# An earlier gate for two loads, and list products queued behind newer work

## The chip, the cores and the metric

The kernel runs on one core of a Trainium2 chip. The metric is the time of one execution on the device in microseconds (us). The engines of the core work through one instruction list each, in order, and wait for one another by semaphores: TensorE (PE) for products and transposes, VectorE (DVE), ScalarE (ACT), GpSimd (POOL), and SyncE (SP), which here only issues DMAs. ScalarE and GpSimd issue DMAs too.

## The reference

A causal convolution along the sequence, then a mixture of experts with one expert per token. In short:

```python
w = softmax(weight, axis=-1)                         # 8 heads, 7 taps
x_pad = concatenate([zeros(B, 6, D), x], axis=1)     # x: 8 x 2880 x 192, float32
x = einsum('hk,bskhg->bshg', w, unfold(x_pad))       # causal, per head of 24 columns
g_idx = argmax(x @ w_group)                          # 4 groups
e_idx = argmax(x[g] @ w_expert[g])                   # 4 experts in the group
h = maximum(x[e] @ w1[g, e], 0)                      # 192 -> 1024
out[e] = g_w * e_w * (h @ w2[g, e])                  # 1024 -> 192, times both softmax weights
```

There are 23040 tokens and 16 experts. Every token is computed by its own expert only, so tokens have to be sorted by expert.

## The kernel before

**Units.** The tokens are cut into blocks of 120, and the blocks into units of 4, 8, 12, 8, 8, 8 blocks for the first two batches and of 12 from then on. I call a unit by its number u in the code, from 0; the eighth and ninth unit are u=7 and u=8.

**Routing of a unit** (`unit`). The block of x (`xin`, or rooms borrowed from weight buffers for u=3 to u=6) is convolved by eight products with a band matrix, one per head (L516). ScalarE copies each result out of its PSUM bank into `xc` (L525). There are three `xc` buffers: u=0 and u=1 share one, u=5 takes it next, u=2's goes to u=6, u=3's to u=7, u=5's to u=8; u=4 sits in a weight buffer. TensorE transposes `xc` (L540, L548), ScalarE copies these as `ta` and `tb` (L541, L549), the logits are products of them with the router weights (L581, L584), and ScalarE copies them to `lg` (L587). VectorE then finds the group and the expert (`mx`, `dd`, `sc`, `oh`, `ohx`, L621 to L633), counts tokens per expert within the unit (`cum`, L641), and writes the token's weight (L652), after which ScalarE issues the store of `xc` to DRAM, `xcd` (L654). Two small products with a triangle and a matrix of ones (`tri`, `ones`, L663, L664) give offsets; VectorE makes places out of them (`off`, `ends`, `pos`, `posn`, `posb`, L667 to L677) and two one-hot matrices `ohl` and `ohr` (L695, L702).

**List products** (`list_products`). One product per block of the unit (L716), with `ohl` as the weights, sorts the token numbers by expert. VectorE turns the result into `lsi` (L724, L726), GpSimd writes it into the table `idtab` (L729). For the first units the list products are put aside and run `LATE` = 8 steps later; at u=4 all that are left are run. With five units in the table, SP reads the first id list (L1228), the weights of the next experts are issued behind it, GpSimd gathers the tokens of the first slots (L816), and the expert products begin (L918, L936, L940).

**Order.** The code runs the stages of several units as generators, a step of one at a time. A scheduling layer then orders each engine's instructions by their dependencies and the order of issue; `hold` and `pin` keep an instruction in the program's order, and `issue_after` puts one behind another. Buffers that rotate add dependencies of their own.

**The gate of x.** Loads of x for u=7 to u=10 are let go late on purpose of the code: a small VectorE memset (L248) writes a corner of the `xin` buffer, and the load on SP's queue has to wait for it. u=8 begins a batch and needs a halo memset (L233) as well. `KX` = 142 is the step in which this happens for u=7 and u=8 together.

Of the kernel before, what the change touches and what calls it, by code (L numbers as in the profile page):

```python
# [24 lines left out]
BI = 2  # L25
# [4 lines left out]
LH = 32  # L30
# [7 lines left out]
def conv_moe_kernel(  # L38
# [10 lines left out]
    nc = tc.nc  # L49
# [41 lines left out]
    for b in range(B):  # L91
        k = b * NB
# [33 lines left out]
    QGB = 3  # L126
    AHEAD = 112
    LISTLAG = 8
    LATE = 8
    HOLD = 2  # L130
    LAG_S = 1
    PTURN = (4, 6)
# [21 lines left out]
    UG = [0, 5, 6, 1, 5, 8, 0, 5, 6, 0, 5, 7, 0, 5, 6, 2, 5, 10]  # L154
    SK = [8, 8, 6, 11, 10, 9, 9]
    KPRE = [60, 150, 155, 160, 162, 110]
    KX = 142
    SEV = 99
    TB = 4
    HGAP = 3  # L160
# [108 lines left out]
    for q, (p0, r0, n) in enumerate(((0, 0, P), (0, P, D2), (D2, P, D2))):  # L269
        c = min(q, 1)  # L270
# [82 lines left out]
    k = 0  # L353
    while k < E:
        n = CAPS.count(CAPS[k])
# [98 lines left out]
    GPIN = (2, 3)  # L454
    ohp_last = [None]
    list_last = [None]
    shared = []
    bands = {}

# [4 lines left out]
    def unit(u, pre=None):  # L464
# [41 lines left out]
        for h in range(H):  # L506
# [6 lines left out]
            else:  # L513
                ops = ((band, xin),)
            for i, (bb, xx) in enumerate(ops):
                nc.tensor.matmul(  # L516
                    out=ps[0:BT, 0:nb * HC], lhsT=bb[0:R, h, :], rhs=xx[0:R, :, cs],
                    start=i == 0, stop=i == len(ops) - 1,
                )
# [56 lines left out]
        def logits_of(q):  # L576
            lgp = bank("l")
            for i in range(HQ):
                o = lgp[0:BT, 2 * i * REPL * NL:2 * (i + 1) * REPL * NL].rearrange("p (j n) -> p j n", j=2)
                for j in range(2):  # L580
                    nc.tensor.matmul(  # L581
                        out=o[:, j].rearrange("p (r n) -> p r n", n=NL), lhsT=ta[:, q, 2 * i + j],
                        rhs=wr[:, 0, 0:NL].unsqueeze(1).broadcast_to([P, REPL, NL]), start=j == 0, stop=False)
                nc.tensor.matmul(  # L584
                    out=o[:, :, 0:NL], lhsT=tb[:, q, i], rhs=wrb[:, :, 0:NL], start=False, stop=True)
            read.add((u, q))
            nc.scalar.activation(  # L587
# [124 lines left out]
        def list_products():  # L712
            pl = bank("l")
            nrep = REPO if u < REPU else 1
            for k in range(nb):
                nc.tensor.matmul(  # L716
                    out=pl[:, 0:nrep * LH].rearrange("p (r n) -> p r n", r=nrep),
                    lhsT=ohl[0:Q, k // BI, :, :, k % BI].rearrange("p e l -> p (e l)"),
                    rhs=ohr[0:Q, k // BI, :, k % BI].unsqueeze(1).broadcast_to([Q, nrep, LH]),
                    start=k == 0, stop=k == nb - 1,  # L720
                )
            lv5 = rt.tile([P, LH], F32, name="lv5", bufs=1)
            lsi = rt.tile([P, LH], I32, name="lsi", bufs=4)
            nc.vector.tensor_scalar(  # L724
# [8 lines left out]
            finished(u)  # L733

        if u < NEED - 1:
            waiting.append((done[0] + LATE, list_products))
        else:
            while waiting:
                waiting.pop(0)[1]()
            list_products()  # L740
# [807 lines left out]
```

## Time and profile before

| what | us |
|---|---|
| median of 3 runs (lowest, highest) | 1089.47 (1089.16, 1090.57) |
| the profiled execution | 1089.97 |
| its span | 1088.1 |
| TensorE busy in it | 1043.7 |
| VectorE, ScalarE, GpSimd busy | 677.6, 618.4, 531.7 |

The profile is of one execution. A time in a view is counted from the start of the span. PE in a view is TensorE's products, PEld its weight loads, PEclk the share of full clock that was granted. In brackets stands how long an engine was idle before an instruction and what ended that. Source lines L in rows of before are lines of the kernel before; in the changed kernel the same lines stand 1 to 5 lines lower.

### The profile page before, as it was taken

How to read it: one execution, taken by the hardware profiler on the slowest of the kernel's cores; microseconds unless marked ns; L12 is line 12 of the kernel's file. 1: busy time of each engine (PE TensorE's matmuls, PEld its weight loads, DVE VectorE, ACT ScalarE, POOL GpSimd, SP SyncE). 2: the span in 40 equal slices, each digit the busy share in tenths (PEclk: the TensorE clock that was granted, in tenths of full speed). 3: DMA queues.
4: the chain of work that ended last, by engine and by line, in shares of the span. 5: the costliest groups of instructions: out<-in, count | busy, mean ns of one | idle time of the engine just before them, and what ended most of it. 6: DMA issues, size and time to landing. Idle time of an engine off the chain costs nothing.

```text
span 1088.1 us, 20687 instructions
## 1 busy us (share of the span) xinstructions
PE 1043.7 (96%) x7116; PEld 980.7 (90%) x7116; DVE 677.6 (62%) x1650; ACT 618.4 (57%) x1380; POOL 531.7 (49%) x677
## 2 busy tenths in 40 slices
PE   6878999999999999999999999999999999999996
PEld 5756888998999899899999999999999999999996
DVE  4667878886777766656464646556466465655652
ACT  5566687886666645545453645545455455555552
POOL 3233343543333446655554553555556656667542
PEclk9989999999999999999999999999999999999998
DMA  8866897886674343432231313133132233233200
GB/s 210 233 174 161 194 271 201 230 224 186 161 167 133 93 116 89 115 85 65 75 83 53 100 41 90 56 95 97 42 96 69 77 92 104 66 87 98 68 26 23
DMA packets 120281, 126.40 MB, mean 116 GB/s; under 512 B 20619, under 2 KB 106896, under 8 KB 120170
## 3 DMA queue, kind: packets, MB, share of 16 engines
q1 hardware_dynamic: 72682, 71.24, 24.7%
q0 software_dynamic: 24160, 35.99, 11.9%
q10 hardware_dynamic: 23328, 17.80, 6.7%
q8 instruction: 57, 0.93, 0.4%
q14 instruction: 54, 0.44, 0.1%
HBM read 89.03 MB, written 36.07 MB: 115 GB/s over the span
## 4 chain that ended last, share of the span: by engine, by line
PE 76%; DMA 7%; DVE 6%; issue 5%; ACT 3%; POOL 3%; POOLq 0%; SPq 0%; ACTq 0%; DVEq 0%
PE ph L888 26%; PE po L902 10%; PE pm L902 7%; PE ph L918 7%; PE po L906 5%; PE po L936 4%; PE pm L906 3%; PE pm L516 3%; PE po L940 2%; DMA out<-ys,idp 2%; DMA xin<-in_x 2%; PE ph L852 1%; POOL out L955 1%; POOL xg L816 1%; PE pm L540 1%
## 5 line engine op out<-in xcount | busy, mean ns | idle before, releaser
L955 POOL DMA_INDIRECT out<-ys,idp x187 | 214.2, 1146 | 258.2 <-DVE ys L965 203.9
L892 DVE SCALAR_TENSOR_TENSOR hl<-ph,hh 128x360 fp32r<-128x360 f32 (+13 forms) x328 | 189.5, 584 | 197.9 <-ACT hh L891 174.8
L891 ACT ACTIVATE hh<-ph 128x360 fp32r<-128x360 f32 (+13 forms) x328 | 166.3, 515 | 207.9 <-PE ph L888 182.4
L816 POOL DMA_INDIRECT xg<-xcd,idp x187 | 226.7, 1212 | 70.6 <-issue 36.6
L902 PE MATMUL po<-cw,hh 128*120 128x384 f32 (+6 forms) x656 | 209.9, 357 | 0.0
L888 PE MATMUL ph<-xa,wf 128*128 128x360 f32 (+13 forms) x656 | 182.3, 359 | 0.0
L888 PE MATMUL ph<-xc,wf 128*128 128x360 f32 (+13 forms) x656 | 176.4, 350 | 1.7 <-DVE xc L864 1.7
L906 PE MATMUL po<-cw,hl 128*120 128x192 f32 (+6 forms) x656 | 164.7, 251 | 0.0
L902 PE MATMUL pm<-cw,hh 128*120 128x384 f32 (+6 forms) x440 | 147.1, 356 | 0.0
L936 PE MATMUL po<-cw,hh 128*128 128x384 f32 x400 | 134.5, 386 | 0.1
L888 PEld LDWEIGHTS ph<-xc,wf 128*128 128x128 f32 x656 | 118.8, 189 | 11.1 <-DVE xc L864 1.9
L906 PEld LDWEIGHTS po<-cw,hl 128*120 128x120 f32 (+6 forms) x656 | 121.7, 186 | 3.0
L918 PE MATMUL ph<-xa,wf 128*128 128x256 f32 x600 | 118.8, 306 | 5.1 <-DVE wf L783 2.2
L902 PEld LDWEIGHTS po<-cw,hh 128*120 128x120 f32 (+6 forms) x656 | 120.4, 184 | 2.8
L888 PE MATMUL ph<-lts,wf 128*128 128x360 f32 (+13 forms) x328 | 115.0, 351 | 0.0
L906 PE MATMUL pm<-cw,hl 128*120 128x192 f32 (+6 forms) x440 | 110.4, 251 | 0.0
L888 PEld LDWEIGHTS ph<-xa,wf 128*128 128x128 f32 x656 | 100.9, 189 | 1.3
L940 PE MATMUL po<-cw,hl 128*128 128x192 f32 x400 | 101.6, 254 | 0.0
L918 PEld LDWEIGHTS ph<-xa,wf 128*128 128x128 f32 x600 | 88.7, 192 | 11.6 <-DVE wf L783 2.4
L924 DVE SCALAR_TENSOR_TENSOR hl<-ph,hh 128x512 fp32r<-128x512 f32 x100 | 68.2, 686 | 44.0 <-ACT hh L923 38.2
L918 PE MATMUL ph<-xb,wf 128*128 128x256 f32 x400 | 81.9, 286 | 2.8 <-DVE xb L864 2.0
L923 ACT ACTIVATE hh<-ph 128x512 fp32r<-128x512 f32 x100 | 59.5, 598 | 43.6 <-PE ph L918 40.1
(277 smaller groups left out, 1905.2 us busy)
## 6 DMA issues: line engine op xcount, KB each, us to landing
rawc<-in_moe_w SPq DMA_DIRECT2D x66, 384.0 KB
raw<-in_moe_w SPq DMA_DIRECT2D x33, 512.0 KB
xcd<-xc ACTq DMA_DIRECT2D x13, 1085.6 KB
raw<-in_moe_w SPq DMA_DIRECT2D x33, 256.0 KB
xin<-in_x SPq DMA_DIRECT2D x7, 1134.0 KB
xin<-in_x SPq DMA_DIRECT2D x5, 1039.5 KB
xg<-xcd,idp POOLq DMA_INDIRECT x187
out<-ys,idp POOLq DMA_INDIRECT x187
```

Of the source, the lines that this page charges most:

```text
L816: nc.gpsimd.indirect_dma_start(out=xs[t][0:m, 0:XW], out_offset=None, in_=xcd[0:known, :], in_offset=bass.IndirectOffsetOnAxis(ap=ids[0:m, ...
L888: nc.tensor.matmul(out=hp, lhsT=W[wgt][:, fs], rhs=xx[:, 0:n], start=i == 0, stop=i == len(ops) - 1)
L891: nc.scalar.activation(out=hh, in_=hp, func=AF.Relu)
L892: nc.vector.scalar_tensor_tensor(out=hl, in0=hp, scalar=0.0, in1=hh.bitcast(F32), op0=ALU.max, op1=ALU.subtract,)
L902: nc.tensor.matmul(out=oo[t][0:m, 0:2 * D], lhsT=hh[:, ts], rhs=cw[:, f].rearrange("p a d -> p (a d)"), start=f == 0, stop=False,)
L906: nc.tensor.matmul(out=oo[t][0:m, 0:D], lhsT=hl[:, ts], rhs=cw[:, f, 0, :], start=False, stop=f == NF - 1,)
L918: nc.tensor.matmul(out=hp[:, j], lhsT=wgt[:, fs], rhs=xx, start=i == 0, stop=i == len(ops) - 1)
L923: nc.scalar.activation(out=hh, in_=hp, func=AF.Relu)
L924: nc.vector.scalar_tensor_tensor(out=hl, in0=hp, scalar=0.0, in1=hh.bitcast(F32), op0=ALU.max, op1=ALU.subtract,)
L936: nc.tensor.matmul(out=oo[t][:, 0:2 * D], lhsT=hh[:, j, ts], rhs=cw[:, f].rearrange("p a d -> p (a d)"), start=f == 0, stop=False,)
L940: nc.tensor.matmul(out=oo[t][:, 0:D], lhsT=hl[:, j, ts], rhs=cw[:, f, 0, :], start=False, stop=f == NF - 1,)
L955: nc.gpsimd.indirect_dma_start(out=outviews[nscat[0] % len(outviews) if view is None else view], out_offset=bass.IndirectOffsetOnAxis(ap=i ...
```

## The change

`KX` goes from 142 to 130, so that the two gate memsets are issued twelve steps earlier. `LATE` becomes a table: the list products of u=2 are put aside for 14 steps, those of u=3 for 10. And with `BEHIND` the list products of u=1 are issued after the last logits product that was recorded by then, those of u=2 and u=3 after the last logits and the last convolution product.

```diff
--- before.py
+++ after.py
@@ -126,7 +126,8 @@
     QGB = 3
     AHEAD = 112
     LISTLAG = 8
-    LATE = 8
+    LATE = (8, 8, 14, 10)
+    BEHIND = ((), ("l",), ("l", "c"), ("l", "c"))
     HOLD = 2
     LAG_S = 1
     PTURN = (4, 6)
@@ -154,7 +155,7 @@
     UG = [0, 5, 6, 1, 5, 8, 0, 5, 6, 0, 5, 7, 0, 5, 6, 2, 5, 10]
     SK = [8, 8, 6, 11, 10, 9, 9]
     KPRE = [60, 150, 155, 160, 162, 110]
-    KX = 142
+    KX = 130
     SEV = 99
     TB = 4
     HGAP = 3
@@ -454,6 +455,7 @@
     GPIN = (2, 3)
     ohp_last = [None]
     list_last = [None]
+    recent = {}
     shared = []
     bands = {}
 
@@ -513,7 +515,7 @@
             else:
                 ops = ((band, xin),)
             for i, (bb, xx) in enumerate(ops):
-                nc.tensor.matmul(
+                recent["c"] = nc.tensor.matmul(
                     out=ps[0:BT, 0:nb * HC], lhsT=bb[0:R, h, :], rhs=xx[0:R, :, cs],
                     start=i == 0, stop=i == len(ops) - 1,
                 )
@@ -581,7 +583,7 @@
                     nc.tensor.matmul(
                         out=o[:, j].rearrange("p (r n) -> p r n", n=NL), lhsT=ta[:, q, 2 * i + j],
                         rhs=wr[:, 0, 0:NL].unsqueeze(1).broadcast_to([P, REPL, NL]), start=j == 0, stop=False)
-                nc.tensor.matmul(
+                recent["l"] = nc.tensor.matmul(
                     out=o[:, :, 0:NL], lhsT=tb[:, q, i], rhs=wrb[:, :, 0:NL], start=False, stop=True)
             read.add((u, q))
             nc.scalar.activation(
@@ -712,13 +714,16 @@
         def list_products():
             pl = bank("l")
             nrep = REPO if u < REPU else 1
-            for k in range(nb):
-                nc.tensor.matmul(
-                    out=pl[:, 0:nrep * LH].rearrange("p (r n) -> p r n", r=nrep),
-                    lhsT=ohl[0:Q, k // BI, :, :, k % BI].rearrange("p e l -> p (e l)"),
-                    rhs=ohr[0:Q, k // BI, :, k % BI].unsqueeze(1).broadcast_to([Q, nrep, LH]),
-                    start=k == 0, stop=k == nb - 1,
-                )
+            with ExitStack() as queued:
+                for kind in BEHIND[u] if u < len(BEHIND) else ():
+                    queued.enter_context(tc.issue_after(recent[kind].ins))
+                for k in range(nb):
+                    nc.tensor.matmul(
+                        out=pl[:, 0:nrep * LH].rearrange("p (r n) -> p r n", r=nrep),
+                        lhsT=ohl[0:Q, k // BI, :, :, k % BI].rearrange("p e l -> p (e l)"),
+                        rhs=ohr[0:Q, k // BI, :, k % BI].unsqueeze(1).broadcast_to([Q, nrep, LH]),
+                        start=k == 0, stop=k == nb - 1,
+                    )
             lv5 = rt.tile([P, LH], F32, name="lv5", bufs=1)
             lsi = rt.tile([P, LH], I32, name="lsi", bufs=4)
             nc.vector.tensor_scalar(
@@ -733,7 +738,7 @@
             finished(u)
 
         if u < NEED - 1:
-            waiting.append((done[0] + LATE, list_products))
+            waiting.append((done[0] + LATE[u], list_products))
         else:
             while waiting:
                 waiting.pop(0)[1]()
```

What this does to the order of the instructions, at three places. Buffer numbers are kept here, since the places differ in them.

ScalarE, around the last evictions of u=4 (`cw_643`), before. `xc_787` is the buffer of u=5, `lg_547` the logits of u=3, and the DMA row is the store of u=2. In brackets stands what an instruction waits for; DMAHW is a transfer, at `xc_787` the stores of u=0 and u=1, which had its buffer before.

```order
L525 ACTIVATE cw_643<-ph_754 120x8x24 [waits PE_49]
L525 ACTIVATE cw_643<-pm_668 120x8x24 [waits PE_49]
L654 DMA xcd_87<-xc_352 120x12x193 [waits DMAHW2_49,DVE_49]
L587 ACTIVATE lg_547<-pm_671 120x80 [waits PE_49]
L525 ACTIVATE cw_643<-pm_682 120x8x24 [waits PE_49]
L525 ACTIVATE cw_643<-pm_724 120x8x24 [waits PE_49]
L526 ACTIVATE cw_643<-cw_643 120x4x64 [waits Activation_49]
L541 ACTIVATE ta_231<-pm_759 128x480 [waits PE_49]
L627 ACTIVATE dd_686<-dd_686 120x160 [waits DVE_49]
L549 ACTIVATE tb_232<-po_765 128x240 [waits PE_49]
L541 ACTIVATE ta_231<-pm_791 128x480 [waits PE_49]
L525 ACTIVATE xc_787<-pm_797 120x8x24 [waits DMAHW6_49,DMAHW5_49,PE_49]
```

The same place in the changed kernel, where u=5 is `xc_769`:

```order
L527 ACTIVATE cw_643<-po_715 120x8x24 [waits PE_49]
L527 ACTIVATE cw_643<-ph_754 120x8x24 [waits PE_49]
L527 ACTIVATE xc_769<-ph_770 120x8x24 [waits DMAHW6_49,DMAHW5_49,PE_49]
L527 ACTIVATE cw_643<-pm_668 120x8x24 [waits PE_49]
L656 DMA xcd_87<-xc_352 120x12x193 [waits DMAHW2_49,DVE_49]
L589 ACTIVATE lg_547<-pm_671 120x80 [waits PE_49]
L527 ACTIVATE cw_643<-pm_682 120x8x24 [waits PE_49]
```

The first eviction of u=5, which waits for the stores of u=0 and u=1, stood behind the transposes of u=4 and now stands ahead of the eviction of u=4 from `pm_668`, of the store of u=2 and of the logits of u=3.

VectorE, the gate of x (`MEMSET xin`), before. `cum_899`, `cw_643` and `off_966` belong to u=4, `wf` is a weight split.

```order
L650 TENSOR_SCALAR sg_888<-ss_885 120x8
L641 SCALAR_TENSOR_TENSOR cum_899<-keep8_132,ohx_895 120x128
L248 MEMSET xin_901 1x2
L248 MEMSET xin_904 1x2
L233 MEMSET xin_904 6x192
L649 TENSOR_REDUCE se_887<-pick_886 120x8
L651 SCALAR_TENSOR_TENSOR se_887<-se_887,sg_888 120x8
L783 TENSOR_TENSOR wf_204<-raw_475,wf_204 128x1024
L652 RECIPROCAL cw_643<-se_887 120x8
L667 TENSOR_TENSOR off_966<-ph_963,eoff_155 128x16
```

In the changed kernel, where the rows around it belong to u=2 (12 blocks) and the `RECIPROCAL` to u=3:

```order
L654 RECIPROCAL xc_434<-se_691 120x8
L679 TENSOR_SCALAR posb_737<-posn_234 120x12
L249 MEMSET xin_842 1x2
L249 MEMSET xin_845 1x2
L682 SCALAR_TENSOR_TENSOR posh_739<-posb_737,posn_234 120x12
L685 TENSOR_SCALAR row8_741<-posb_737 120x12
L234 MEMSET xin_845 6x192
L693 TENSOR_TENSOR oh8_743<-row8_741,iol_152 120x96
L704 TENSOR_TENSOR ohr_747<-ior_158,posh_739 120x384
```

The three memsets moved from behind the `cum` of u=4 into the list steps of u=2, and the weight split has left this place.

TensorE, the second half of the logits of u=4 (`ta_231`, `tb_232`), before. The first two rows are the end of the list products of u=3 (`ohl_819`).

```order
L716 LDWEIGHTS ohl_819
L716 MATMUL pm_848<-ohr_820,ohl_819 128x192
L581 MATMUL pm_865<-wr_104,ta_231 120x100 x2
L584 MATMUL pm_865<-wrb_233,tb_232 120x2x20
L581 MATMUL pm_865<-wr_104,ta_231 120x100 x2
L584 MATMUL pm_865<-wrb_233,tb_232 120x2x20
L516 MATMUL pm_873<-wf_199,band_214 120x192
```

In the changed kernel, from the end of the list products of u=2 (`ohl_746`) on:

```order
L721 LDWEIGHTS ohl_746
L721 MATMUL ph_782<-ohr_747,ohl_746 128x192
L665 LDWEIGHTS tri_121
L665 MATMUL ph_800<-cum_703,tri_121 128x16
L666 LDWEIGHTS ones_119
L666 MATMUL ph_800<-cum_703,ones_119 128x16
L550 MATMUL ph_827<-ident_112,cw_643 128x120 x2
L518 MATMUL ph_853<-wf_199,band_214 120x192
L586 MATMUL pm_859<-wrb_233,tb_232 120x2x20
L583 MATMUL pm_859<-wr_104,ta_231 120x100 x2
L586 MATMUL pm_859<-wrb_233,tb_232 120x2x20
L518 MATMUL ph_884<-wf_199,band_214 120x192
```

The logits of u=4 stood behind the list products of u=3 and now stand ahead of them; two of their products stand even ahead of the list products of u=2. The tri and ones products of u=3 follow those list products directly. Further on, one convolution of u=6 that stood just ahead of tri and ones of u=4 now stands behind them. SP's order is the same in both kernels. The last difference on TensorE is at the list products of u=5, where two transposes now stand ahead of them; from there on its order is the same.

## Rows read from the trace of the kernel before

**Rows 1.** The page, busy time of each engine in us (share of span), instructions

```profile
PE 1043.7 (96%) x7116; PEld 980.7 (90%) x7116; DVE 677.6 (62%) x1650; ACT 618.4 (57%) x1380; POOL 531.7 (49%) x677
```

**Rows 2.** Windows: stretch, length, busy us per engine (instructions), PEclk, DMA share, GB/s

```profile
48.00:52.00 4.00, 2.34 (x21) 1.91 (x20) 2.52 (x13) 0.91 (x3) 0.19 (x1) 1.00 0.85 215
64.00:68.00 4.00, 0.12 (x1) 0.15 (x1) 2.59 (x13) 2.14 (x6) 0.18 (x1) 0.89 1.01 323
68.00:72.00 4.00, 4.00 (x16) 3.10 (x17) 1.26 (x3) 0.52 (x2) 0.33 (x1) 0.50 0.96 317
96.00:100.00 4.00, 2.30 (x12) 1.95 (x11) 3.16 (x14) 0.58 (x2) 2.35 (x3) 0.73 0.61 151
100.00:104.00 4.00, 4.00 (x34) 3.95 (x33) 1.72 (x3) 2.36 (x6) 2.33 (x3) 0.84 0.95 224
300.00:1088.00 788.00, 774.43 (x5090) 741.16 (x5088) 460.73 (x1012) 413.53 (x925) 419.53 (x528) 0.99 0.31 83
```

**Rows 3.** Chain of waits, 60 to 100 us: start, length, what

```profile
60.92 6.83 DMA xin<-in_x
```

**Rows 4.** Timeline of TensorE: start, duration, operation, [idle before <- releaser]

```profile
50.48 1.17 PE L716 MATMUL ph<-ohr,ohl 120*128 120x192 f16 x12 [1.66 <-DVE ohl L695]
...
55.59 0.84 PE L716 MATMUL pm<-ohr,ohl 120*128 120x192 f16 x8 [1.25 <-DVE ohl L695]
...
57.48 0.56 PE L516 MATMUL pm<-wf,band 126*120 126x192 f32 x2
...
60.77 0.65 PE L516 MATMUL po<-wf,band 126*120 126x288 f32 x2
61.26 0.19 PE L663 MATMUL ph<-cum,tri 120*128 120x16 bf16 x1
...
67.88 1.28 PE L516 MATMUL ph<-xin,band 126*120 126x288 f32 x2 [4.46 <-DMA xin<-in_x]
68.96 1.49 PE L716 MATMUL pm<-ohr,ohl 120*128 120x192 f16 x8
...
74.77 0.57 PE L540 MATMUL pm<-ident,xc 120*128 120x120 f32 x4
...
98.21 1.01 PE L918 MATMUL ph<-xa,wf 128*128 128x256 f32 x3 [1.70 <-DVE xa L858]
```

**Rows 5.** Timeline of VectorE, 46 to 70 us

```profile
48.21 0.13 DVE L677 TENSOR_SCALAR posb<-posn 120x12 f32<-120x12 f32 x1
...
57.95 0.32 DVE L621 TENSOR_REDUCE mx<-lg 120x40 f32<-120x160 f32 x1 [1.06 <-ACT lg L587]
...
60.80 0.07 DVE L248 MEMSET xin<- 1x2 f32 x2
...
62.60 0.12 DVE L667 TENSOR_TENSOR off<-ph,eoff 128x16 f32<-128x16 f32 x1
...
66.11 0.69 DVE L695 TENSOR_TENSOR ohl<-ohp,oh 120x1024 f16<-120x1024 f16 x1
```

**Rows 6.** DMA queue of the stores, 68 to 72 us: packets, MB, share

```profile
q10 hardware_dynamic: 786, 0.60, 46.7%
```

**Rows 7.** DMA queue of the stores, 43.0 to 43.2 us

```profile
q10 hardware_dynamic: 1, 0.00, 0.3%
```

**Rows 8.** DMA queue of the stores, 83.4 to 83.6 us

```profile
q10 hardware_dynamic: 3, 0.00, 3.5%
```

**Rows 9.** Timeline of ScalarE, 30 to 86 us (ACTq: a DMA issue)

```profile
32.20 0.33 ACTq L654 DMA_DIRECT2D xcd<-xc  x1
...
43.86 0.24 ACT L587 ACTIVATE lg<-pm 120x80 f32<-120x80 f32 x1 [0.86 <-PE pm L584]
...
46.93 0.35 ACT L525 ACTIVATE xc<-pm 120x192 f32<-120x192 f32 x1
...
84.97 0.42 ACT L525 ACTIVATE xc<-ph 120x288 f32<-120x288 f32 x1 [0.71 <-DMA xcd<-xc]
```

**Rows 10.** DMA queues, 32 to 37 us: SP's queue

```profile
q1 hardware_dynamic: 904, 1.15, 105.7%
```


## The prediction

> **What bounds the kernel now.** I read the page's totals first, then the windows by stage, the chain of waits up to 100 us, and last the timelines of the engines and the DMA queues around the place of the change. The page [rows 1] gives TensorE 1043.7 us busy in a span of 1088.1 us. The windows [rows 2] show where the idle 44 us are: from 300 us on TensorE is busy 774.43 of 788 us at a granted clock of 0.99, so nothing but less TensorE work shortens that part; before it there are holes. The largest is at 64 to 68 us, with 0.12 us of work, and the next stretch, 68 to 72 us, runs at a granted clock of 0.50, the lower of the two levels (1.2 GHz), because of it. The chain [rows 3] goes through the load of x that ends this hole: issued at 60.92, 6.83 us long. On TensorE [rows 4] the convolution of u=7 starts at 67.88 after 4.46 us of waiting for it. The load was let go by the memset at 60.80 [rows 5]. Routing work of this kind has to be done before the first expert product, which runs freely from 98.21 [rows 4]. What follows 98 us stands in the same order in both kernels and its loads and waits hang on events inside it, so I count the change as the shift of that point.
>
> **The change part by part.** No instruction is added or removed in the routing; four things move.
>
> The gate (KX). The two memsets for x of u=7 and u=8, and the halo memset, stand behind the posb of u=2, at 48.21 [rows 5], no longer behind the cum of u=4. SP's order is the same, so the load goes some 11 us earlier, at about 50 with the delay below. It now runs beside the stores of u=2 and u=3. Alone it took 6.83 us, at 323 GB/s where it ran best [rows 2, 3]. Where a load and a store shared the engines, the stores moved 0.60 MB in 4 us [rows 6], about half of that rate; at half rate all the way 1.134 MB take 3.5 us more, and x is there by 60.3. TensorE asks for it at about 62.6. The wait of 4.46 us goes. The two memsets take VectorE 0.07 us each [rows 5], the halo one is wider; I take 0.3 us for all, on the way to the list of u=2.
>
> The first eviction of u=5 on ScalarE. This one works against the change. Its convolution now precedes the list products of u=1, and its eviction stands before the last evictions of u=4. It writes the buffer of u=0 and u=1, so it waits for the store of u=1. In the kernel before that wait was over when ScalarE came to it. The store's last packet is at 43.0 to 43.2 [rows 7]. For the time from there to the release I take the store of u=5: last packets at 83.4 to 83.6 [rows 8], ScalarE goes on at 84.97 [rows 9], so 1.4 us. ScalarE is therefore held until about 44.6. Then come this eviction, one of u=4 and a DMA issue, 1.0 us together (the issue is 0.33, and I take the evictions alike), and only then the logits copy that stood at 43.86 [rows 9]: about 45.6, 1.7 us late. VectorE's steps for u=2 and u=3 alternate from that copy on, one behind the other, up to the list of u=2. Bounds: 0, if the store is in time (a gain is excluded, since the logits copy waits for nothing that this eviction frees); and 4.0, if the release came only at 46.93, where the first eviction of u=5 went through without a wait before [rows 9]. I take 1.7, from the nearest row of the same kind. By the Trainium skill (DMA: Bandwidth & Descriptors, section Anatomy of one DMA — SWDGE (gpsimd) path) a DMA has about 2 us of fixed cost, most of it the receipt of the last write; taken for this store, issued by ScalarE's queue, the wait would be 0.6 us longer and the gain below 0.6 us smaller.
>
> The list products of u=2 to u=4. The list of u=2 comes at 50.48 + 1.7 + 0.3 = 52.5 [rows 4]. The tri and ones of u=3 now follow at once. A third of the second logits of u=4 was put before it; the rest needs a transpose after it. Before, list, logits and copy of the logits took 57.95 - 55.59 = 2.4 us, of these 0.7, 1.2 and 0.5. Now it is list 1.0 (1.17 with overlap), 0.8 for two thirds of the logits, 0.5 for the copy, and 1.2 for tri, transposes and their copy, an estimate by the same rows: VectorE's mx of u=4 is at 56.0 and no longer at 57.95 [rows 5]. It is placed inside the list chain of u=3, so that list pays: VectorE reaches it 1.7 us late, mx and dd add 0.6 (0.32 each), and a short wait for the copy 0.2: 55.59 becomes 58.1 on TensorE [rows 4]. From there to the next convolution the kernel before needed 57.48 - 55.59 = 1.9 us, list 0.7 and logits 1.2; the logits are now gone from between. One convolution, 61.26 - 60.77 = 0.49 us, is moved behind tri. So: list 0.7, then 61.26 - 57.48 - 0.49 = 3.3 us, and tri of u=4 is at 62.1 (before 61.26 [rows 4]). VectorE's off follows at 62.25, where it was held to 62.60 by a weight split ahead of it [rows 5]. From off to ohl 3.5 us (62.60 to 66.11; one weight split lies inside in both kernels), ohl itself 0.7: the list of u=4 at 66.5. Before it stood at 68.96, behind the wait for x. Gain here 2.45 us. TensorE waits some 1.7 us for it, where it waited 4.46.
>
> The clock. From that list to the transposes of u=6 the kernel before needed 74.77 - 68.96 = 5.8 us [rows 4]. The same work at the upper level is list and logits 1.9 and three convolutions of 0.49: 3.4 us. Without the long hole I take the upper level: 69.9, a gain of 4.9 us.
>
> What is given back. The weights of the next experts wait for the id list, which follows the list of u=4 and moves with it, by about 2.9 us (its products, now at the upper level, end that much earlier). The store of u=5 queues behind these weights and holds ScalarE to 84.97 [rows 9]: that point moves to about 82.0, 2.9 us and not 4.9. But a weight copy, a logits copy and two copies of transposes (some 2 us) now stand before that wait, so little of the difference is lost; I take 0.3 us. Left: 4.6 us at 98.21 and at the end.
>
> At nothing: the cast ohp of u=4 ahead of a table write on GpSimd (that write is read only when the last of five is in), the moved memory clear on ScalarE (it is needed by the second expert), the swapped rows of VectorE in the list of u=5. They are hidden by the waits of these engines there; uncovered each costs its own length, and the clear, out of the way where ScalarE is busy, may as well give its own.
>
> Sum: 2.45 (list) + 2.45 (clock) - 0.3 = 4.6 us. The profiled execution took 1089.97 us, its span is 1088.1 and 1.9 lie around it; 1089.97 - 4.6 = 1085.4. That execution was 0.5 us above the median of the three runs, 1089.47, so I give 1085.0.
>
> **The rivals.**
> - A, the store is in time: the eviction of u=5 is not held, the 1.7 us are not lost, and the gain is 6.3 us: 1083.3. For it: the wait is inferred from one other store's 1.4 us. Against: packets until 43.2 are seen [rows 7], and ScalarE now comes to this eviction before it has finished u=4.
> - B, the clock falls elsewhere. One long hole becomes several short ones (at 44, 51, 66 and 82 us). For it: at 96 to 104 us a hole of 1.70 us [rows 4] went with a granted clock of 0.73 and 0.84 [rows 2], 4 x 0.27 + 4 x 0.16 = 1.7 us lost. Against: 48 to 52 us, with 2.34 of 4 us busy, kept 1.00. Price 1.7 to 2.4 us, gain about 2.5: 1087.0. The Trainium skill (TensorE: Matmul & The Clock Gate, section A second HAM failure mode: psum-queue depth-cycling) says that frequent short idling between groups of products can make the clock swing; the holes at 48 to 52 speak against it, those at 96 to 104 for it.
> - C, the stores lose to the loads, slower than before. SP's queue can keep ScalarE's waiting: at 32 to 37 us it had 105.7% of the engines [rows 10] and the store issued at 32.20 [rows 9] nothing. The store of u=2, now issued near 45.1, needs 1.09 MB at 0.16 MB/us or better: out by 51.9, released by 53.3. If x of u=7 and u=8, at the engines from 51, is served first, what is left of it waits for 2.26 MB at 0.32 MB/us, 7.1 us: released at about 59.9, where the first eviction of u=6 wants it at 55.7. That is 4.2 us on everything behind, the list of u=4 at 70.7 with the hole and the low clock back: about 1.7 us slower, 1091.2. It decides from a release after 55.7 on; each us beyond costs one.
> - D, the gain does not reach the end: the weight loads after 100 us set the pace and the shift is eaten there, 0 to 1 us left: 1089.0. For it: DMA share 0.95 at 100 to 104 [rows 2]. Against: each such load waits for a buffer that TensorE's stage frees, and moves with it. If the change did not take the wait away at all, it would be the same time.
>
> **How the numbers follow.** Forecast 0.46, A 0.20, B 0.16, C 0.08, D 0.10. About 0.2% (2.2 us) is what a measurement of this kernel can tell from no change. Faster by more: forecast, A and most of B, 0.79; within it: the rest of B and D, 0.13; slower: C, 0.08. The range takes in A with a gain of up to 7.6 us and ends where D begins, 1081.8 to 1088.4; C, most of D and little else are left out, 0.2.
>
> **What would show it.** Right: the x load issued near 50; no wait for it on TensorE; ScalarE idle until about 44.6 with the store of u=1 as the releaser; the list of u=4 near 66.5; a granted clock near 1.00 at 68 to 76; the first free expert product near 93.6. Wrong: ScalarE not held at 44 (A); a granted clock under 0.9 between 50 and 90 (B); ScalarE held past 56 by the store of u=2 (C); the product at 93.6 and the end not earlier (D).

## The result, and the profile after

The changed kernel took 1081.66 us (median of 6 runs, 1080.44 to 1084.61), the kernel before, in turn with it, 1090.09 us (6 runs, 1089.16 to 1092.17). The ratio is 0.9915, with a 95% interval of 0.9894 to 0.9937: by the medians 8.4 us faster, where 4.6 were forecast. That is just below the low end of the range, 1081.8. The ratio on record is not the quotient of the two medians: by it the gain is 9.3 us (6.9 to 11.6). The gains of the experiments below go by the ratio. On two more chips the ratio was 0.9921 (0.9900 to 0.9943) and 0.9898 (0.9873 to 0.9924).

The page of the changed kernel, busy time of each engine [rows 1]:

```profile
PE 1040.6 (96%) x7116; PEld 979.8 (91%) x7116; DVE 676.0 (63%) x1650; ACT 618.3 (57%) x1380; POOL 534.9 (50%) x677
```

TensorE is busy 3.1 us less, for the same products, and the span is 8.8 us shorter. The windows show where, in the columns of [rows 2]:

```profile
48.00:52.00 4.00, 2.58 (x24) 2.19 (x23) 2.52 (x16) 0.94 (x4) 0.19 (x1) 1.00 0.71 142
60.00:64.00 4.00, 2.70 (x18) 2.07 (x16) 3.86 (x16) 3.95 (x9) 1.21 (x2) 1.00 1.03 246
64.00:68.00 4.00, 3.97 (x31) 3.58 (x32) 3.29 (x8) 2.73 (x9) 0.00 (x0) 1.00 0.36 101
68.00:72.00 4.00, 3.96 (x27) 3.07 (x25) 2.09 (x10) 3.54 (x12) 2.51 (x2) 1.00 0.22 48
84.00:88.00 4.00, 2.06 (x16) 1.57 (x15) 3.60 (x8) 3.11 (x8) 0.38 (x2) 0.97 0.76 201
88.00:92.00 4.00, 2.73 (x12) 2.28 (x12) 3.17 (x14) 0.53 (x2) 2.34 (x3) 0.50 0.51 128
92.00:96.00 4.00, 4.00 (x27) 3.92 (x27) 1.59 (x3) 1.91 (x4) 2.34 (x3) 0.68 0.95 223
```

The stretch that had 0.12 us of work has 3.97, and the half clock behind it (0.50 and 0.76 from 68 to 76 us) is gone. The low clock that before lay at 96 to 104 us (0.73 and 0.84) now lies at 88 to 96 (0.50 and 0.68). TensorE's timeline has the steps of [rows 4]:

```profile
50.45 1.18 PE L721 MATMUL ph<-ohr,ohl 120*128 120x192 f16 x12 [1.35 <-DVE ohl L697]
...
55.52 0.85 PE L721 MATMUL pm<-ohr,ohl 120*128 120x192 f16 x8 [0.59 <-DVE ohl L697]
...
59.52 0.19 PE L665 MATMUL ph<-cum,tri 120*128 120x16 bf16 x1
...
60.39 0.72 PE L518 MATMUL ph<-xin,band 126*120 126x288 f32 x2
...
64.03 0.84 PE L721 MATMUL pm<-ohr,ohl 120*128 120x192 f16 x8 [1.25 <-DVE ohl L697]
...
67.45 0.57 PE L542 MATMUL pm<-ident,xc 120*128 120x120 f32 x4
...
90.22 1.01 PE L923 MATMUL ph<-xa,wf 128*128 128x256 f32 x3 [1.27 <-DVE xa L863]
```

The convolution of u=7 at 60.39 waits for nothing. The list products of u=4 come at 64.03 (before 68.96), the transposes of u=6 at 67.45 (74.77), the first free expert product at 90.22 (98.21). VectorE, to be held against [rows 5]:

```profile
48.10 0.12 DVE L679 TENSOR_SCALAR posb<-posn 120x12 f32<-120x12 f32 x1
48.28 0.07 DVE L249 MEMSET xin<- 1x2 f32 x2
...
53.87 0.32 DVE L623 TENSOR_REDUCE mx<-lg 120x40 f32<-120x160 f32 x1
...
59.78 0.17 DVE L669 TENSOR_TENSOR off<-ph,eoff 128x16 f32<-128x16 f32 x1 [1.50 <-PE ph L666]
...
63.29 0.68 DVE L697 TENSOR_TENSOR ohl<-ohp,oh 120x1024 f16<-120x1024 f16 x1
```

The gate's memset is where the order said, and `mx` of u=4 is 4 us earlier. ScalarE, around 43 us and at the two points that wait for a store [rows 9]:

```profile
43.24 0.34 ACT L527 ACTIVATE xc<-ph 120x192 f32<-120x192 f32 x1 [3.12 <-DMA xcd<-xc]
...
43.72 0.24 ACT L589 ACTIVATE lg<-pm 120x80 f32<-120x80 f32 x1
...
70.23 0.32 ACTq L656 DMA_DIRECT2D xcd<-xc  x1
...
77.41 0.43 ACT L527 ACTIVATE xc<-ph 120x288 f32<-120x288 f32 x1
```

At 43.24 ScalarE is released by the store of u=1, 1.4 us before the 44.6 of the forecast, and its logits copy still comes at 43.72 (before 43.86). At 77.41 the first eviction of u=8 waits for no store (84.97 before). The queue of the stores from 42.8 to 43.0 us, its last packet before that release [rows 7]:

```profile
q10 hardware_dynamic: 1, 0.00, 0.3%
```

SyncE's queue: the first part of x for u=7 and u=8, and the id list:

```profile
48.40 0.34 SPq L237 DMA_DIRECT2D xin<-in_x  x1
...
70.41 0.39 SPq L1233 DMA_DIRECT2D idp<-idtab  x1
```

The store of u=5 (70.23, in ScalarE's rows) went out 0.18 us ahead of the id list. In the kernel before it went out 3.96 us behind it:

```profile
74.15 0.39 SPq L1228 DMA_DIRECT2D idp<-idtab  x1
```

```profile
78.11 0.32 ACTq L654 DMA_DIRECT2D xcd<-xc  x1
```

### The profile page after: what moved, and what is told of

Same layout as the page of the kernel before. It is cut to its first block, busy times and chain, and to the rows that moved or that the text cites. A ratio compares the mean times of both kernels' runs of the same rounds, so it can differ in the third digit from the quotient of the medians.

```text
span 1079.3 us, 20687 instructions
## 1 busy us (share of the span) xinstructions
PE 1040.6 (96%) x7116; PEld 979.8 (91%) x7116; DVE 676.0 (63%) x1650; ACT 618.3 (57%) x1380; POOL 534.9 (50%) x677
## 4 chain that ended last, share of the span: by engine, by line
PE 85%; DVE 5%; DMA 4%; ACT 3%; issue 2%; POOL 0%; SPq 0%; POOLq 0%; ACTq 0%; DVEq 0%
PE ph L893 28%; PE po L907 10%; PE ph L923 10%; PE pm L907 8%; PE po L941 6%; PE po L911 5%; PE pm L911 4%; PE pm L518 3%; PE po L945 3%; DMA out<-ys,idp 2%; PE pm L542 1%; PE ph L857 1%; DMA xin<-in_x 1%; PE pm L721 1%; ACT wf L792 1%
## 5 line engine op out<-in xcount | busy, mean ns | idle before, releaser
L929 DVE SCALAR_TENSOR_TENSOR hl<-ph,hh 128x512 fp32r<-128x512 f32 x100 | 68.1, 685 | 43.2 <-ACT hh L928 42.9
```

The costliest lines, as they stand in the source:

```text
L929: nc.vector.scalar_tensor_tensor(out=hl, in0=hp, scalar=0.0, in1=hh.bitcast(F32), op0=ALU.max, op1=ALU.subtract,)
```

## The experiments

From one profiled run to the next the whole program stands up to 5 us earlier or later: the list products of u=2 began between 48.20 and 53.40 us, for the first load of x takes longer in some runs than in others (13.05 us in the chain of the kernel before, 12.03 to 15.86 where the chains of others go through the same load). So I count the places in a trace from that product on. The first free expert product is the one at 98.21 in [rows 4], the first that runs on without long waits. The last column is the end of the span.

| profile | list u=4 | transposes u=6 | first free expert product | end |
|---|---|---|---|---|
| before | 18.48 | 24.29 | 47.73 | 1037.6 |
| changed, first | 13.58 | 17.00 | 39.77 | 1028.8 |
| changed, second | 13.61 | 17.03 | 40.41 | 1033.3 |
| changed, third | 13.66 | 17.08 | 39.36 | 1029.6 |
| gate alone (KX 130) | 15.27 | 18.69 | 44.43 | 1032.3 |
| gate alone (KX 118) | 15.01 | 18.43 | 42.08 | 1029.4 |
| lists alone | 15.88 | 20.23 | 43.11 | 1030.9 |
| list ahead of x | 16.37 | 21.84 | 47.69 | 1037.2 |
| hole filled, before | 16.67 | 20.56 | 44.40 | 1033.7 |
| no hold | 13.57 | 16.99 | 39.19 | 1028.3 |
| store behind | 13.59 | 17.01 | 40.14 | 1024.9 |

Up to the transposes of u=6 the three profiles of one kernel agree within 0.1 us; behind them they do not, and the end differs by 4.5 us. Medians are therefore needed for the end, and even their intervals are 2 us to each side.

**The gate alone.** The kernel before with one number changed.

```diff
-    KX = 142
+    KX = 130
```

> The kernel before with KX = 130 and nothing else: list products as before. Theory T (the wait for x and the low clock behind it are the main cost, and the order of the lists is worth something by itself): the 4.46 us wait of TensorE for x goes, the granted clock at 64 to 76 us is near 1.00, but the list products of u=4 still stand behind the logits of u=4 and after the first convolution of u=7. Gain 4.5 to 5.5 us against before, first free expert product near 93. Rival G (the gate is everything): 8 to 8.5 us, as much as the whole change. Rival L (the lists are everything): 0 to 1 us.

Measured: 1082.59 us against 1089.62, ratio 0.9940 (0.9919 to 0.9961), 6.5 us faster (4.2 to 8.8), where 4.5 to 5.5 were expected. The profiled run was the longest of eight (1087.47). ScalarE at the first eviction of u=8:

```profile
84.88 0.42 ACT L525 ACTIVATE xc<-ph 120x288 f32<-120x288 f32 x1 [2.04 <-DMA xcd<-xc]
```

It had 2.04 us to wait for the store of u=5, which was issued 2.42 us behind the id list. So what the prediction called given back exists in this kernel, and the release is 3.0 us earlier than before (84.88 - 53.40 against 84.97 - 50.48), where 2.9 was forecast for the whole change. A low clock followed (0.91 and 0.66 from 84 to 92 us, 1.7 us lost).

**The gate alone, earlier still.** `KX = 118`, otherwise the same.

> The kernel before with KX = 118: the gate alone again, but some 4 us earlier still than with 130; TensorE, ScalarE, GpSimd and SP have the same order as with 130. Theory (once x is there in time more haste is worth nothing, and the store of u=5 gives part of the gain back): the same as the gate alone within 1.5 us, the first eviction of u=8 on ScalarE again held by the store of u=5, for about 2 us, released 10.7 to 11.7 us after the id list's issue. Rival (the load now takes the engines from the store of u=1 and the first weights, and something before 50 us is late): 1 us or more slower than the gate alone.

Measured: 1082.92 against 1089.60, ratio 0.9955 (0.9933 to 0.9977), 4.9 us faster (2.5 to 7.3). The same row:

```profile
79.14 0.42 ACT L525 ACTIVATE xc<-ph 120x288 f32<-120x288 f32 x1 [1.36 <-DMA xcd<-xc]
```

The two gate kernels agree within their intervals. Here the clock stayed at 1.00 from 84 to 92 us, and the first expert product is 2.35 us earlier than with 130: 0.7 us of that is the shorter hold and 1.7 us the clock.

**The lists alone.** The changed kernel with the gate back at 142.

```diff
-    KX = 130
+    KX = 142
```

> The changed kernel with KX = 142 again: the list products in their new order, the gate memsets behind the cum of u=4. Theory T: that cum is itself some 3 us earlier now (near 57.5), so x lands near 64.4, TensorE waits for it 1 to 2 us and not 4.46, and the clock falls less; the list products of u=4 near 65. Gain 5 to 6.5 us; so this and the gate alone add up to more than the whole change (8.4 us), since either one takes away most of the same wait. Rival S (the effects add up): the gate's gain and this one sum to 8.4 us. Rival G (the gate is everything): 0 to 1 us.

Measured: 1084.99 against 1089.62, ratio 0.9960 (0.9945 to 0.9976), 4.4 us faster (2.6 to 6.0), where 5 to 6.5 were expected. TensorE's convolution of u=7:

```profile
65.35 1.29 PE L518 MATMUL ph<-xin,band 126*120 126x288 f32 x2 [3.28 <-DMA xin<-in_x]
```

The wait for x is 3.28 us and not 1 to 2, for x was issued at 57.77 and took 7.45 us (before 6.83). At the transposes of u=6 the gate gives 5.6 (5.9 with 118), the lists 4.1, and both 7.3 us: 2.4 to 2.6 us overlap, since either edit shortens the same hole. Of the overlap 1.5 us are clock: from the list of u=4 to these transposes it takes 5.81 us before, 3.42 with the gate, 4.35 with the lists and 3.42 with both. The other 0.9 to 1.1 us are the wait ahead of the list.

At the end the two gains add up to 10.9 us (9.3 with KX 118), the whole change gains 8.4 to 9.3; with 2 us on each that neither shows the overlap nor excludes that the gains add. The rival that the lists are everything falls by the gate's gain. The rival that the gate is everything falls by the lists' 4.4 us, where it had 0 to 1, and by the places up to the transposes; the gate's own interval reaches the whole gain.

**The list ahead of the wait for x.** The kernel before; only the list products of u=4 no longer stand behind the convolution that waits for x.

```diff
+    with tc.issue_after(recent["p4"].ins) if (u, h) == (7, 0) else nullcontext():
         nc.tensor.matmul(out=ps[0:BT, 0:nb * HC], lhsT=bb[0:R, h, :], ...)
...
+                recent["p%d" % u] = nc.tensor.matmul(   # list products
```

> The kernel before, gate and lists in the old order, but the first convolution of u=7 is issued behind the list products of u=4, so that these no longer stand behind the wait for x. The hole before that convolution stays, only behind the list. Theory T: the list products start near 66.9, as soon as ohl is ready (68.96 in before), so VectorE and the id list are 2 us earlier, but TensorE is still without work from about 63.4 to 66.9, the clock still falls, and the convolutions are late: gain 1 to 2.5 us. Rival (the list's own place decides, the clock costs nothing): gain above 4 us. Rival (only the x wait of the convolutions decides): no change.

Measured: 1089.73 against 1089.62, ratio 0.9997 (0.9978 to 1.0016): no gain, 2.4 us at most, where 1 to 2.5 were expected. The list is 2.1 us and the transposes of u=6 2.45 us earlier, as expected, and then ScalarE:

```profile
83.04 0.42 ACT L527 ACTIVATE xc<-ph 120x288 f32<-120x288 f32 x1 [4.03 <-DMA xcd<-xc]
```

Its wait for the store of u=5 grew from 0.71 to 4.03 us, and took all of it: the release is 34.43 us behind the list of u=2, in the kernel before 34.49. This is the give-back of the prediction at full size.

**The hole filled, in the kernel before.** Eight more products ahead of the convolution that waits for x.

```diff
+            for _ in range(8 if (u, h) == (7, 0) else 0):
+                nc.tensor.matmul(out=ps[0:BT, 0:nb * HC], lhsT=band[0:R, h, :],
+                    rhs=loaded[6][0:R, :, cs], start=True, stop=True)
```

> The kernel before with eight more products (band with x of u=6, into the bank that the first convolution of u=7 overwrites) ahead of that convolution, in the 4.46 us in which TensorE waits for x. The wait for x stays, the work behind it should run at the upper level of the clock. Prediction's clock term: the list products of u=4 start when they did, the transposes of u=6 come 2.45 us earlier, near 72.3. What of it reaches the end: by the theory of the store of u=5 next to nothing, since the id list is only 0.7 us earlier and ScalarE is released 10.7 to 11.7 us after it: 0 to 1 us faster than before. Rival (the clock's gain goes through): 2 to 2.5 us faster. Rival (the clock has other causes than the hole): granted clock at 68 to 72 still near 0.5, no change anywhere.

Measured: 1086.62 against 1089.60, ratio 0.9975 (0.9960 to 0.9991): 2.7 us faster (1.0 to 4.4), with more work. The scheduling layer also put the convolution behind the list products, so the kernel to compare with is the one just above. Its windows and, below, those of the kernel above:

```profile
64.00:68.00 4.00, 4.00 (x20) 3.11 (x19) 3.79 (x18) 3.38 (x8) 0.18 (x1) 1.00 0.93 294
68.00:72.00 4.00, 4.00 (x31) 3.38 (x30) 1.43 (x4) 1.98 (x4) 0.60 (x1) 1.00 0.97 309
```

```profile
64.00:68.00 4.00, 3.02 (x14) 2.61 (x15) 2.08 (x5) 0.81 (x4) 0.33 (x1) 0.61 0.99 319
68.00:72.00 4.00, 4.00 (x26) 3.36 (x25) 1.73 (x6) 3.88 (x10) 0.86 (x2) 0.97 0.62 205
```

The granted clock stays at 1.00 where it was 0.61 and 0.97. From the list to the transposes of u=6 it takes 3.89 and not 5.47 us, in the kernel before 5.81. So the clock term of the prediction is shown, at 1.6 to 1.9 us here and 2.4 in the changed kernel (5.81 to 3.42). My expectation that the store would take it all was wrong: the store was issued only 0.49 us behind the id list here, and 2.42 in the kernel above. It released ScalarE 7.65 us behind the id list here and 11.31 there. So only 1.3 of the 3.3 us between the two kernels at the first free expert product are there at the transposes of u=6; the others come with the store.

**No hold.** The changed kernel, the first convolution of u=5 behind the list products of u=1, so that its eviction no longer precedes the logits copy.

```diff
+    with tc.issue_after(recent["p1"].ins) if (u, h) == (5, 0) and "p1" in recent else nullcontext():
         recent["c"] = nc.tensor.matmul(...)
...
+                    recent["p%d" % u] = nc.tensor.matmul(   # list products
```

> The changed kernel, with the first convolution of u=5 issued behind the list products of u=1, so that its eviction on ScalarE no longer stands ahead of the logits copy of u=3. It tests the term of 1.7 us in the prediction. The prediction's reading: 1.7 us faster than the changed kernel. The reading of the profile after (the store of u=1 was in by 43.24 us, the logits copy not late): no change, within 0.5 us of the changed kernel, the logits copy of u=3 at 43.7 as there.

Measured: 1081.82 against 1089.62, ratio 0.9928 (0.9905 to 0.9951), no faster than the changed kernel (0.9915), where the prediction's reading was 1.7 us; intervals of 2 us to each side do not settle that alone. ScalarE:

```profile
42.86 0.24 ACT L590 ACTIVATE lg<-pm 120x80 f32<-120x80 f32 x1 [0.86 <-PE pm L587]
```

The logits copy now waits for the logits product on TensorE, as in the kernel before, and from the list of u=1 to that of u=2 it takes 9.39 us, in the changed kernel 9.20. In these profiles the hold costs nothing that can be measured. It is not always free. In the kernel with 17 and 20 added products below, whose order is the same up to here, the profile has the list of u=1 at 41.00 and on ScalarE:

```profile
43.87 0.33 ACT L528 ACTIVATE xc<-ph 120x192 f32<-120x192 f32 x1 [3.99 <-DMA xcd<-xc]
...
44.34 0.24 ACT L590 ACTIVATE lg<-pm 120x80 f32<-120x80 f32 x1
```

The logits copy is 3.34 us behind the list of u=1 (2.47 in the changed kernel), and the list of u=2 is 10.08 us behind it, 0.9 us late.

**The store behind the id list.** The changed kernel, the store of u=5 four steps later, two rows on ScalarE.

```diff
+        yield from [None] * (4 * (u == 5))
         (nc.sync if u >= SEV else SE).dma_start(out=xcw, in_=xc[0:BT, 0:nb, 0:XW])
-        for _ in range(rest):
+        for _ in range(rest - 4 * (u == 5)):
```

> The changed kernel, with the store of u=5 issued four steps later: on ScalarE it stands behind two more copies, every other row of every engine is where it was. It is then issued near 71.4 us, some 1.0 us behind the id list (70.41), where the changed kernel issued it 0.18 us ahead. Theory (the order of these two decides what the gain is worth): in the runs where the store was 2.4 to 4.0 us behind the id list, ScalarE's first eviction of u=8 was released 10.7 to 11.7 us after the id list was issued. So it is released at 81.1 to 82.1, not at 77.41; 3.5 to 4.5 us of the gain go, the median is 1085 to 1086 us, and ScalarE's row names the store as its releaser. Rival (the store would be in time anyway, the 4.6 us that the prediction left over were only undersized elsewhere): within 1 us of the changed kernel, no wait for the store.

Measured: 1080.72 against 1089.60, ratio 0.9934 (0.9913 to 0.9954): 7.2 us faster than before (5.0 to 9.5), from the changed kernel not to be told apart, with a lower median and a higher ratio. SyncE's id list, then ScalarE's store and the eviction:

```profile
67.17 0.39 SPq L1233 DMA_DIRECT2D idp<-idtab  x1
```

```profile
68.58 0.32 ACTq L656 DMA_DIRECT2D xcd<-xc  x1
...
76.81 0.42 ACT L527 ACTIVATE xc<-ph 120x288 f32<-120x288 f32 x1 [1.69 <-DMA xcd<-xc]
```

The store is 1.41 us behind, the hold 1.69 us, and the first expert product 0.4 us later than in the first profile of the changed kernel and earlier than in the second. The second profile of the changed kernel itself had the store behind the list (1.68 us, hold 0.69). My theory that this order is worth 3.5 to 4.5 us falls by the place of this product; the times alone, with 2 us to each side, could not say it.

What the order does is seen over all profiles: issued within 0.2 us of the id list the store held nobody; 0.49 us behind it, it released ScalarE 7.65 us after that list, 1.41 behind 9.6, 1.68 behind 10.2, and 2.4 to 4.0 behind 10.7 to 11.8. The first free expert product comes 0.3 to 1.2 us later with it: at 39.19 to 39.77 where nothing was held (twice the changed kernel, and no hold), at 40.10 to 40.41 with the store 1.4 to 1.7 us behind. The clock differs between these profiles too, so not all of that need be the store.

**Holes filled in the changed kernel.** First nine, then 20 products ahead of the first expert product; and, in a third kernel, 17 there and 20 ahead of the second expert's first product.

```diff
+    def dummies(k, hp, ah):      # called ahead of the first expert product
...
+        with tc.issue_after(recent["t"].ins):
+            for _ in range(20):
+                nc.tensor.matmul(out=hp[:, 0], lhsT=ah[:, 0:P], rhs=ah[:, 0:SLOT], start=True, stop=True)
```

> The changed kernel with nine more products (weights with weights, into a bank that the first expert product overwrites) in the 1.92 us hole of TensorE ahead of the first expert product. There the changed kernel runs 88 to 96 us at a granted clock of 0.50 and 0.68. Theory (what the clock loses is caused by holes, as at 64 to 72 us in the kernel before): the clock stays near 1.00 and the work of 88 to 96 us (2.73 us busy at 0.50, 4 us at 0.68) takes 1.4 + 1.3 = 2.6 us less; with the second hole of 1.27 us not filled I expect 1 to 2.6 us, a median of 1079 to 1081. Rival (the next hole pulls the clock down anyway): 0 to 0.5 us.

> The changed kernel with 17 more small products (a constant matrix with itself, into a bank that the next product overwrites) ahead of the first expert product, and 20 ahead of the first product with the second expert's weights, where TensorE waits 2.16 us for a weight split on VectorE (116.03 us in the changed kernel). Theory (chance decides after which hole the clock falls, and that is most of what differs between two runs of one kernel): in the changed kernel's profile 84 to 96 us lost 3.3 us to the clock and 112 to 128 us 3.4 us, in the kernel with the later store the second loss was 0 after the same hole. With both holes filled neither loss occurs: granted clock 0.95 or more in both stretches, median 2 to 5 us below the changed kernel, 1077 to 1080 us. Rival (the added products delay the real ones, or the clock falls at the next hole): within 1.5 us of the changed kernel, or slower.

> The changed kernel with 20 more products (weights with weights, some 2.5 us) ahead of the first expert product, enough for both holes there (0.9 to 1.9 and 1.3 to 1.6 us); the order on the other engines is as in the changed kernel, on TensorE four transposes of u=8 move behind the first four expert products. Theory: the granted clock from 84 to 96 us stays at 0.95 or more, as with all holes filled, and without the new waits that the reordering cost there: 1.5 to 3.3 us (what the changed kernel's three profiles lost to the clock there) below the changed kernel of this call. Rival (what the clock gives back is taken by the products themselves, since VectorE and ScalarE set the pace at the first expert): within 1.5 us of it.

Measured: with nine 1082.44 (ratio 0.9939, 0.9914 to 0.9964); with 17 and 20, 1090.91 against 1084.71 for the changed kernel beside it; with 20, 1081.71 against 1082.19. None is better than the changed kernel, where 1 to 5 us had been expected of them. With nine the second hole was left, and 88 to 96 us had a clock of 0.75 and 0.83. With 20 the windows and the first free expert product are:

```profile
88.00:92.00 4.00, 3.58 (x30) 3.36 (x29) 3.83 (x14) 2.09 (x6) 1.30 (x2) 1.00 0.66 171
92.00:96.00 4.00, 3.75 (x33) 3.53 (x32) 2.31 (x6) 1.96 (x5) 3.08 (x4) 1.00 0.79 176
```

```profile
91.57 0.62 PE L923 MATMUL ph<-xa,wf 128*128 128x256 f32 x3 [0.42 <-DVE xa L863]
```

The clock stays at 1.00. Around the first expert products each of the twelve other profiles, without these additions or with the nine, lost 1.7 to 3.4 us to the clock, and the two with both holes filled none, so the holes were its cause there too. But 91.57 is 40.19 us behind the list of u=2, no earlier than without: VectorE's `xa` sets that point, and TensorE's faster products wait for it. The third kernel kept 1.00 from 40 to 128 us as well; its added products changed the order on the other engines, and one new wait is nearly as long as what it lost against the changed kernel, 6.2 us. TensorE's wait, in us, times, longest, and behind it ScalarE's for a weight load:

```profile
PE pm L551 <- ACT xc L529: 5.1, 1, 5.1
```

```profile
136.67 0.84 ACT L801 ACTIVATE cw<-rawc 128x768 fp32r<-128x768 f32 x1 [7.65 <-DMA rawc<-in_moe_w]
```

That this wait comes from the changed order is likely and not shown.

**The changed kernel twice more,** beside these two.

> The changed kernel once more, beside the one with filled holes on the same chip: to compare these two directly, and for a second profile. Theory (chance decides at which hole the clock falls): the first 85 us as in the first profile, the list products of u=4 near 13.6 us and the first free expert product near 39.8 to 40.1 us after the list products of u=2; the low-clock stretches behind 84 us may lie elsewhere, and the total may differ by 3 us for that alone. Median 1080 to 1083.5 us.

> The changed kernel once more, beside the one with 20 more products. Median 8 to 9.5 us below the kernel before of this call, as twice before (ratio 0.9915 and 0.9921).

Measured: 1084.71 against 1093.32 and 1082.19 against 1092.81, 8.6 and 10.6 us faster by the medians; the first median and the second gain lie above what was expected, as do the 40.41 us of the second profile. The positions are in the table.

## Why the prediction was wrong in size

Its direction, the wait that goes and the order of the steps were right. By its own steps:

- **The gate: right.** x was issued at 48.40 (about 50 forecast) and TensorE does not wait for it. The memsets were to cost 0.3 us; from the list of u=1 to that of u=2 the three profiles of the changed kernel need 9.20, 9.12 and 9.30 us, before 9.04. So memsets and hold together cost 0.1 to 0.3 there.
- **The hold of ScalarE by the store of u=1: the step that failed.** "ScalarE is therefore held until about 44.6" and "1.7 us late" came to a release at 43.24 and a copy at 43.72. I took 1.4 us from a last packet to a release from the store of u=5 [rows 8, 9], whose end lay among GpSimd's gathers (their queue at 122% of the engines from 83.4 to 83.6). For u=1 it is at most 0.44 us (last packet in 42.8 to 43.0). From the release to the copy it is 0.48 us where I had 1.0. And the copy had slack, since its product is not ready earlier: it ends at 43.63. One row was not enough for this delay. For the store of u=5 it is 0.6 to 1.5 us in the nine profiles that show ScalarE held by it, and mine was the longest. For the store of u=1 it is 0.3 to 0.5 us in five profiles, and 0.7 to 0.8 and 1.1 to 1.2 in two more, with no gathers there; so the traffic does not explain it alone. That the hold was free is in part luck: in the first profile it ended just in time for the copy, and in the one shown under No hold it ended 0.9 us too late. The sentence from the Trainium skill (DMA: Bandwidth & Descriptors, Anatomy of one DMA — SWDGE (gpsimd) path), some 2 us with the receipt, was further off still; this trace does not agree with it for this store, which ScalarE's queue issued.
- **The list products: the order of events right, 0.45 us undersized.** Without the 2.0 us of hold and memsets the list of u=4 was forecast 4.45 us early; it is 4.90 early (18.48 to 13.58). The 0.5 us that `mx` and `dd` of u=4 were to cost between the lists of u=2 and u=3 did not come: 5.07 us, before 5.11. `mx` of u=4 is at 53.87, tri of u=4 at 59.52.
- **The clock: right,** 2.45 forecast, 7.29 - 4.90 = 2.39 measured at the transposes of u=6, and shown by filling the hole.
- **The give-back: its size was off, and its sign.** -0.3 was forecast; from the transposes of u=6 to the first free product the three profiles gain 0.1 to 1.2 us over before (first profile 22.77 against 23.44). In the first and the third profile the store went out beside the id list and held nothing, where ScalarE had waited 0.71 us before; in the second it held ScalarE for 0.69 us, and the gain there is the 0.1. So the point that I moved to 82.0, the release of ScalarE, fell away: I had the store queue behind the weights in any case. That its place behind the id list decides the release is borne out by all profiles above. What a hold is worth is only in part shown: it took all of the 2.45 us with the list ahead of x, and 0.3 to 1.2 us at most where the store was 1.4 to 1.7 us behind.
- **Sum.** From the list of u=1 to the first free expert product: 4.90 + 2.39 + 0.67 - 0.16 = 7.8 us, against 4.6. Of the 3.2 us between them 1.8 are the hold and the memsets, 0.5 the lists, 1.0 the give-back, and -0.1 the clock. With the term of the hold alone put right, the forecast would have been A's 1083.3, so the give-back and the lists have their part in the miss. The profile's span is 8.8 us shorter, the median 8.4, and the ratio makes 9.3. What the last 0.6 to 1.5 us are stays open: behind 98 us the runs of one kernel differ by more.

Of the rivals, A (the store is in time) is what happened in effect: ScalarE was held and lost nothing by it. A's 6.3 us still lack the 0.45 of the lists, the memsets and the give-back. B is half there: the low clock at 88 to 96 us loses 3.3 us in the first profile and 1.7 in the second and, from 92 to 100 us, in the third, where 96 to 104 lost 1.7 before; so at most 1.6 us more, of a gain that is larger. C did not occur: the store of u=2 held nobody. D did not: the shift reaches the end.

## What to carry to other kernels

Give the delay between a transfer's last packet and its release a range, here 0.3 to 1.5 us, from several rows; I put the middle of the range where one unlike row was. Where an instruction is held, ask whether what stands behind it was ready at all: a hold that ends when the next operand arrives is free. When two edits shorten the same hole, they share its wait and the clock behind it, so count each once; and when a later wait hangs on another event than the one that moves, as here the store behind the id list, the gain may be gone by then, wholly or not at all.

## What the runs showed of the hardware

Whether a hole costs clock is not the same from run to run. In all three profiles of the changed kernel TensorE waits 2.16 us for a weight split near 115 us. The windows of the first, then of the second:

```profile
112.00:116.00 4.00, 1.50 (x8) 0.83 (x6) 4.00 (x13) 3.91 (x6) 3.08 (x4) 0.88 0.21 72
116.00:120.00 4.00, 3.97 (x20) 3.64 (x21) 2.16 (x5) 0.00 (x0) 1.98 (x2) 0.50 0.67 168
120.00:124.00 4.00, 4.00 (x23) 3.67 (x22) 2.02 (x3) 2.69 (x5) 1.01 (x1) 0.77 1.01 251
```

```profile
112.00:116.00 4.00, 1.54 (x10) 1.07 (x10) 4.00 (x13) 3.27 (x4) 3.16 (x3) 1.00 0.22 74
116.00:120.00 4.00, 4.00 (x35) 3.79 (x33) 2.56 (x6) 1.73 (x4) 2.37 (x3) 1.00 0.85 205
120.00:124.00 4.00, 4.00 (x29) 3.49 (x28) 3.60 (x9) 3.85 (x7) 0.00 (x0) 1.00 1.10 209
```

With 1.50 and 1.54 us of work in the stretch with the hole, the next stretch was granted 0.50 in one run and 1.00 in the other; 0.50 and 0.77 over 8 us are 2.9 us, a third of what the whole change gains. The Trainium skill (TensorE: Matmul & The Clock Gate, A second HAM failure mode: psum-queue depth-cycling) says that frequent short idling can make the clock swing. The traces show such a swing behind a single wait of 2.16 us, and add that the same wait need not cause one. More work can be faster: eight products without use took 2.7 us off the kernel before, with the list products of u=4 moved ahead, which alone gained nothing.
